# Metering the background matmuls by PSUM group, earlier modulation rows, and a branch place of its own for each engine, in a fused adaLN attention and MLP kernel

## The chip, the cores and the metric

The kernel runs on one NeuronCore of a Trainium2 chip. The metric is the device time of one execution in microseconds (us). Engines are named as the profile names them: PE (matmuls; PEld is its weight load), ACT, DVE, POOL, and SP, which here only issues DMAs.

## The reference, cut to what matters

A transformer block on 2048 rows of 512 values: a modulated layer norm, 32 query heads on 8 cached key/value heads over the last 512 cache positions, an output projection, a second modulated layer norm and a ReLU MLP. Six modulation vectors come from one small vector `c`.

```
mod = (silu(c) @ w_mod).reshape(6, 512)          # sa, ca, ga, sb, cb, gb
h = layernorm(x) * (1 + ca) + sa
q = (h @ wq) per head;  k, v = last 512 rows of the caches, one per 4 heads
o = softmax(q k^T / sqrt(128)) v
x = x + ga * (concat(o) @ wo)                    # wo: 4096 x 512
h = layernorm(x) * (1 + cb) + sb
return x + gb * (relu(h @ w1) @ w2)              # w1: 512 x 1792
```

## The kernel before, in words

**Units and steps.** The rows are cut into four blocks of 512. A unit `u` is one head of one block, 128 in all. A program loop over steps `s` (line 1588 on) writes the instructions of all engines in order; no scheduler moves them later. In step `s` PE gets: half of the scores of unit `s` (`s_mms`, into psS), the query projection of unit `s+1` (`q_mms`, psQ), the other half of the scores, then probabilities times values for unit `s-1` (`pv_mms`, psO), then up to four pieces of background work (`pop_bg(4)`, line 1601). ACT copies the query projection out and takes the exponentials. DVE normalises each unit's output (`rinv`, then `o`, lines 1471 and 1472), and SP transposes it with a DMA into one of 22 buffers `oT`. Below, "pv of step s" is the sixteen psO matmuls that stand in step s.

**Background work.** Eight heads make a pass of the output projection. When unit `u` closes a pass, `wo_ready` gets it for step `u+2`, and `enqueue_wo` puts four groups on the queue `bgq`. A group is eight matmuls `psW<-wo,oT`, one for each head, that accumulate in the one PSUM bank psW, followed by an evacuation: DVE copies or adds psW into `acc` (lines 1492 and 1494). Each entry of `bgq` is one matmul, or one evacuation (in the set `evacs`). `mods2`, called at step 20, puts the rest of the modulation there: a row of four matmuls and its copy to `gaf`, one entry of 32 one-column matmuls and its copies to `modc`, and another row and its copy to `gbf`. They all use psW too. Because psW is one bank, a new group's first matmul waits until DVE has emptied it.

`pop_bg(n)` counts matmul entries only; evacuations are free, and it goes on after one:

```
while bgq and (n > 0 or bgq[0] in evacs):
    f = bgq.popleft()
    f()
    n -= f not in evacs
```

**Loads.** `add(step, fn)` puts a load or a layer-norm piece at a step. SP issues its DMAs in program order, and one that has to wait holds all behind it. The modulation weights 2 to 5 are loaded at steps 9, 11, 13 and 15 (line 1572). At steps 60 and 64 the MLP weights are loaded, each in two halves into the space of the modulation weights; the second half is a later writer of the same space and waits for the first to land. The layer norm of blocks 2 and 3 and the second layer norm of blocks 0 and 1 run close to each other and share `xn` and `xnT`.

**The tail.** The MLP is a list `mlp` of groups: `h1_group` (four matmuls into one of the four psS banks, then ACT's ReLU) and `y_group` (fourteen matmuls into psQ or psO, then two DVE operations and the output DMA). After the loop, the left background work and the last pass are mixed with the first `h1` groups, then come the last layer norm and the check value `flag` (line 1652). At line 1678 the place is noted at which all five engines branch: each waits for `flag`, loads it into a register (line 1718), compares and branches (line 1719) either to a general kernel, which did not run here, or to the rest of the fast kernel, which stands behind the general one.

Of the kernel before, what the change touches and what calls it, by code (L numbers as in the profile page):

```python
# [1197 lines left out]
def build_fast(nc, es, top, A_x, A_k_cache, A_v_cache, A_wq, A_wo, B_x, B_w1, B_w2, c, w_mod, out, flag):  # L1198
# [9 lines left out]
    NB = Sq // QB  # L1208
# [71 lines left out]
    kb = KB(nc)  # L1280
    PE = kb.stream("pe", sem("s_pe"))
    ACT = kb.stream("act", sem("s_act"))
    DVE = kb.stream("dve", sem("s_dve"))
    POOL = kb.stream("pool", sem("s_pool"))
    SP = kb.stream("sp", sem("s_sp"))
# [6 lines left out]
    def dma(out_ap, in_ap, key, reads=(), writes=(), transpose=False, eng=None):  # L1292
        k = dsem(key)
        if transpose:
            return kb.op(SP, lambda e: e.dma_start_transpose(out_ap, in_ap), reads=reads, writes=writes, dma_sem=k)
        return kb.op(eng or SP, lambda e: e.dma_start(out_ap, in_ap), reads=reads, writes=writes, dma_sem=k)  # L1296
# [13 lines left out]
    R_rinv, R_vmax, R_chk, R_good, R_flag = Res("rinv"), Res("vmax"), Res("chk"), Res("good"), Res("flag")  # L1310
# [22 lines left out]
    def load_wm(sl, eng=None):  # L1333
        dma(wm[sl], w_mod[:, sl * D:(sl + 1) * D].rearrange("(c p) n -> p c n", p=P), f"wm{sl}", writes=[R_wm[sl]], eng=eng)
# [100 lines left out]
    def pop_bg(n):  # L1435
        while bgq and (n > 0 or bgq[0] in evacs):
            f = bgq.popleft()
            f()
            n -= f not in evacs

    evacs = set()

# [4 lines left out]
    def q_mms(u):  # L1447
        b, h = units[u]
        order = CC_ORDER if u == 0 else range(DC)
        for i, cc in enumerate(order):  # L1450
            mm(bank[QBK], wq_sb[:, cc, h * Dh:(h + 1) * Dh], hT[b % 2][:, cc, :], i == 0, i == DC - 1,
               [R_wq[h], R_hT[b % 2][cc]], [QBK], i == DC - 1)
        kb.op(ACT, lambda e: e.activation(qT[u % NQT][:, :], bank[QBK], ACTF.Copy), reads=[R_b[QBK]], writes=[R_qT[u % NQT]])  # L1453

    def s_mms(u, pr):
        b, h = units[u]
        g = h // R
        for i in range(2):
            kc = pr * 2 + i
            mm(s_ps[pr][:, i, :], kT_sb[:, g, kc * P:(kc + 1) * P], qT[u % NQT][:, :], True, True, [R_kT[g], R_qT[u % NQT]], [kc], i == 1)  # L1460
        kb.op(ACT, lambda e: e.activation(PT[u % NPT][:, pr * 2:pr * 2 + 2, :], s_ps[pr][:, :, :], ACTF.Exp, scale=scale),  # L1461
              reads=[R_b[pr * 2], R_b[pr * 2 + 1]], writes=[R_PT[u % NPT][pr]])
# [43 lines left out]
    def add(step, fn):  # L1506
        tasks.append((step, len(tasks), fn))
        tasks.sort(key=lambda x: x[:2])

    def run_tasks(step, n):  # L1510
        while tasks and tasks[0][0] <= step and n > 0:
            tasks.pop(0)[2]()
            n -= 1
# [55 lines left out]
    for j in range(NPASS):  # L1569
        add(HQ * j + 4, lambda j=j: load_wo(j))  # L1570
    for i, sl in enumerate((2, 3, 4, 5)):
        add(9 + 2 * i, lambda sl=sl: load_wm(sl))
    for b in range(1, NB):
        add(H * b - 20, lambda b=b: load_x(b))
        add_ln(b, 1, H * b - 15)
# [5 lines left out]
    def mods2():  # L1581
        mod_row(0)
        fs = mod_cols_mm(1, WBK)
        bgq.append(lambda: [f() for f in fs] and None)
        evac(lambda: mod_cols_evac(1, WBK))
        mod_row(1)

    for s in range(NU):
        run_tasks(s, 100)
        if s == 20:  # L1590
            mods2()
        if wo_ready and wo_ready[0][0] <= s:
            _, b_, j_ = wo_ready.popleft()
            enqueue_wo(b_, j_)
        s_mms(s, 0)
        if s + 1 < NU:
            q_mms(s + 1)
        s_mms(s, 1)
        if s >= 1:
            pv_mms(s - 1)  # L1600
        pop_bg(4)
# [5 lines left out]
    def h1_group(b, fc):  # L1607
        dst, r = h2_of[b]
        bk = hb_banks[cnt["h"] % len(hb_banks)]
        cnt["h"] += 1  # L1610
        for cc in range(DC):
            mm(bank[bk], w1_sb[:, cc, fc * P:(fc + 1) * P], dst[:, cc, :], cc == 0, cc == DC - 1, [R_w1[fc], r[cc]], [bk], cc == DC - 1)
        kb.op(ACT, lambda e: e.activation(h1T[b % 2][:, fc, :], bank[bk], ACTF.Relu), reads=[R_b[bk]], writes=[R_h1[b % 2][fc]],  # L1613
              pre=all_events(R_wq) if b < 2 else ())

    def y_group(b, tl):
        pt_done = all_events(R_PT[0] + R_PT[1])
        t = b * TPB + tl
        bk = yb_banks[cnt["y"] % len(yb_banks)]
        i = cnt["y"] % NY  # L1620
        cnt["y"] += 1
        for fc in range(FC):
            mm(bank[bk], h1T[b % 2][:, fc, tl * P:(tl + 1) * P], w2_sb[:, fc, :], fc == 0, fc == FC - 1, [R_h1[b % 2][fc], R_w2[fc]], [bk], fc == FC - 1)
        kb.op(DVE, lambda e: e.tensor_tensor(yt[i], bank[bk], gbf[:, :], op=ALU.mult), reads=[R_b[bk], R_gb], writes=[R_yt[i]], pre=pt_done if cnt["y"] <= NY else ())  # L1624
        kb.op(DVE, lambda e: e.tensor_tensor(yo[i], yt[i], x_sb[:, t, :], op=ALU.add), reads=[R_yt[i], R_x[t]], writes=[R_yo[i]])  # L1625
        dma(ov[:, t, :], yo[i], f"y{i}", reads=[R_yo[i]])

    mlp = deque()
    for b in range(NB + 1):
        if b < NB:  # L1630
            mlp.extend(lambda b=b, fc=fc: h1_group(b, fc) for fc in range(FC))
        if b >= 1:
            mlp.extend(lambda b=b, tl=tl: y_group(b - 1, tl) for tl in range(TPB))

    def pop_mlp(n):
        for _ in range(n):
            if mlp:
                mlp.popleft()()
# [27 lines left out]
    b = NB - 1  # L1666
# [7 lines left out]
        ln_norm(b * TPB + tl)  # L1674
    ln_dmaT()
    flag_mm()
    pop_mlp(4)
    cut = {n: (len(t.ops), t.cnt) for n, t in (("sp", SP), ("pe", PE), ("act", ACT), ("dve", DVE), ("pool", POOL))}
    cut_dma = dict(kb.dma_cnt)
    pop_mlp(4)  # L1680
    for cc in range(DC):
        ln_mod_sb(cc, *h2_of[b], 2)
    while mlp:
        pop_mlp(1)
    assert not tasks and not bgq and not wo_ready
    SP.ops.append((lambda e: e.nop(), [(f"y{i}", kb.dma_cnt[f"y{i}"]) for i in range(NY)], []))
    return kb, {"sp": SP, "pe": PE, "act": ACT, "dve": DVE, "pool": POOL}, cut, cut_dma, R_flag.w


def bass_adaLN_cond__sliding_block_cached__dense_activation_relu__prompt_kernel(  # L1690
    nc: bass.Bass,
    A_x: bass.AP,
    A_k_cache: bass.AP,
    A_v_cache: bass.AP,
    A_wq: bass.AP,
    A_wo: bass.AP,
    B_x: bass.AP,
    B_w1: bass.AP,
    B_w2: bass.AP,
    c: bass.AP,  # L1700
    w_mod: bass.AP,
    out: bass.AP,
):
    args = (A_x, A_k_cache, A_v_cache, A_wq, A_wo, B_x, B_w1, B_w2, c, w_mod, out)
    with ExitStack() as top:
        flag = top.enter_context(nc.sbuf_tensor("flag", [1, 8], mybir.dt.int32))
        with ExitStack() as es:
            kb, fast, cut, cut_dma, flag_ev = build_fast(nc, es, top, *args, flag)
            sems = dict(kb.sems)
            meet = top.enter_context(nc.semaphore("s_meet"))  # L1710
        with ExitStack() as es:
            gkb, general = build_general(nc, es, *args)

            def engine(name, e):
                n_ops, n_done = cut[name]
                kb.emit(fast[name], e, 0, n_ops)
                e.wait_ge(sems[flag_ev[0]], flag_ev[1])
                v = e.value_load(flag[0:1, 0:1])
                with e.If(v != 128):
                    if n_done:  # L1720
                        e.wait_ge(sems[name], n_done)
                    if name == "sp":
                        for k, n in cut_dma.items():
                            e.wait_ge(sems[k], n)
                    e.sem_inc(meet, 1)
                    e.wait_ge(meet, len(cut))
                    gkb.emit(general[name], e)
                with e.Else():
                    kb.emit(fast[name], e, n_ops)

            with nc.allow_non_contiguous_dma(reason="tiny c vector load in column layout, value rows of 256 bytes"):
                with nc.Block() as block:
                    @block.sync
                    def _(e):
                        engine("sp", e)

                    @block.tensor
                    def _(e):
                        engine("pe", e)

                    @block.scalar
                    def _(e):
                        engine("act", e)

                    @block.vector
                    def _(e):
                        engine("dve", e)

                    @block.gpsimd
                    def _(e):  # L1750
                        engine("pool", e)
    return nc
# [28 lines left out]
```

## Time and profile before

| What | us |
|---|---|
| median of 3 runs | 658.51 (658.41 to 659.48) |
| the profiled execution, its own time | 660.11 |
| span in its trace, first to last instruction | 658.4 |
| outside the span | 1.7 |
| PE busy in the span | 565.7 (86%) |
| ACT busy / DVE busy / POOL busy | 347.4 / 240.7 / 38.1 |

The engines run side by side, so the columns are not added up. The idle time that stands behind a group of instructions, and what ended it, say where an engine waited; on PE, whose work forms most of the chain that ended last, such a wait is a part of the span. A row of the timeline gives start and duration in us, the engine, the line, the tiles, the count, and in brackets the idle time before it with what ended it.

### The profile page before, as it was taken

What the parts mean: (1) busy time and instruction counts of PE and PEld (TensorE: products, weight loads), DVE (VectorE), ACT (ScalarE), POOL (GpSimd) and SP (SyncE); (2) the same over time, 40 slices, a digit from 0 to 9 for tenths busy, and PEclk for the clock granted to TensorE, in tenths of its full rate; (3) what the DMA queues carried; (4) which work ended last, traced back from release to release, by engine and by line L of the source; (5) the groups of instructions that cost most, each with busy time, mean ns of one, the idle gap of its engine ahead of it and who ended that gap; (6) DMA issues with size and microseconds to landing.
All of it is one profiled execution on the core that took longest, in us unless ns stands there. A gap on an engine that the chain in (4) does not pass through costs nothing.

```text
span 658.4 us, 9730 instructions
## 1 busy us (share of the span) xinstructions
PE 565.7 (86%) x4157; PEld 315.2 (48%) x4157; DVE 240.7 (37%) x531; ACT 347.4 (53%) x445; POOL 38.1 (6%) x40
## 2 busy tenths in 40 slices
PE   3999998888888888888888888888888879699997
PEld 3566555444444445544444444444454444244443
DVE  3343654222225443222235442222233325430324
ACT  1887665555555555555555555555555543415220
POOL 1000000002200100012100000022000000000000
PEclk9999999999999999999999999999999999989999
DMA  9299583111221245511211511111112310300001
GB/s 231 42 206 271 125 176 85 44 32 33 38 60 32 42 81 143 144 33 28 62 33 32 97 33 33 33 27 30 33 33 33 63 27 8 37 18 16 33 16 49
DMA packets 111620, 42.67 MB, mean 65 GB/s; under 512 B 94032, under 2 KB 111184, under 8 KB 111568
## 3 DMA queue, kind: packets, MB, share of 16 engines
q1 hardware_dynamic: 109984, 40.92, 29.1%
q10 hardware_dynamic: 1584, 1.05, 0.5%
q8 instruction: 34, 0.56, 0.4%
q14 instruction: 18, 0.15, 0.1%
HBM read 18.35 MB, written 2.10 MB: 31 GB/s over the span
## 4 chain that ended last, share of the span: by engine, by line
PE 84%; DVE 11%; issue 3%; DMA 1%; ACT 0%; ACTq 0%
PE psS L1350 25%; PE psO L1350 22%; PE psQ L1350 20%; PE psW L1350 17%; DVE o L1472 4%; DVE acc L1494 4%; DVE rinv L1471 2%; DVE acc L1492 1%; DMA wmw<-in_w_mod_dram 1%; PE psS L1353 0%; ACT qT L1453 0%; ACT PT L1461 0%; ACTq L1296 0%; DVE PT L1624 0%; DVE PT L1625 0%
## 5 line engine op out<-in xcount | busy, mean ns | idle before, releaser
L1461 ACT ACTIVATE PT<-psS 128x1024 bf16<-128x1024 f32 x256 | 262.7, 1027 | 207.6 <-PE psS L1350 207.5
L1350 PE MATMUL psW<-wo,oT 128*128 128x512 bf16 x512 | 139.3, 380 | 71.5 <-DVE acc L1494 53.5
L1350 PE MATMUL psS<-qT,kT 128*128 128x512 bf16 x512 | 152.1, 379 | 1.1 <-ACT qT L1453 1.1
L1350 PEld LDWEIGHTS psO<-v,PT 128*128 128x128 bf16 x2048 | 126.6, 98 | 30.2
L1471 DVE RECIPROCAL rinv<-psO 128x4 f32<-128x4 f32 x128 | 23.4, 183 | 317.1 <-PE psO L1350 317.1
L1350 PE MATMUL psO<-v,PT 128*128 128x129 bf16 x2048 | 137.0, 220 | 0.0
L1350 PE MATMUL psQ<-hT,wq 128*128 128x512 bf16 x512 | 131.6, 379 | 0.7 <-DVE hT L1397 0.7
L1350 PEld LDWEIGHTS psW<-wo,oT 128*128 128x128 bf16 x512 | 42.9, 98 | 116.1 <-DVE acc L1494 66.0
L1472 DVE TENSOR_TENSOR o<-psO,rinv 128x512 bf16<-128x512 f32 x128 | 88.5, 691 | 4.5
L1350 PEld LDWEIGHTS psQ<-hT,wq 128*128 128x128 bf16 x512 | 50.1, 98 | 61.4 <-issue 0.9
L1350 PEld LDWEIGHTS psS<-qT,kT 128*128 128x128 bf16 x512 | 49.6, 98 | 59.9 <-issue 1.0
L1453 ACT ACTIVATE qT<-psQ 128x512 bf16<-128x512 f32 x128 | 75.7, 591 | 0.5 <-PE psQ L1350 0.5
L1613 ACT ACTIVATE wq<-psS 128x512 bf16<-128x512 f32 x56 | 33.4, 597 | 61.8 <-PE psS L1350 61.8
L1494 DVE TENSOR_TENSOR acc<-psW,acc 128x512 f32<-128x512 f32 x48 | 32.7, 681 | 9.1 <-PE psW L1350 9.1
L1350 PE MATMUL psS<-h2T,wmw 128*128 128x512 bf16 x112 | 28.6, 411 | 5.1 <-issue 5.1
L1350 PE MATMUL psO<-wmw,wq 128*128 128x512 bf16 x140 | 31.2, 379 | 0.0
L1497 POOL TENSOR_TENSOR acc<-acc,gaf 128x512 f32<-128x512 f32 x12 | 15.2, 1266 | 246.4 <-DVE acc L1494 246.4
L1350 PE MATMUL psS<-hT,wmw 128*128 128x512 bf16 x112 | 24.5, 379 | 0.0
L1366 POOL TENSOR_TENSOR rstd<-rstd,cst 128x4 f32<-128x4 f32 x8 | 8.1, 1013 | 281.6 <-DVE rstd L1365 281.6
L1360 DVE BATCH_NORM_STATS2 st<-x 128x6 f32<-128x512 bf16 x32 | 21.7, 677 | 1.5 <-DMA x<-in_A_x_dram 1.5
L1624 DVE TENSOR_TENSOR PT<-psO,gbf 128x512 f32<-128x512 f32 x10 | 6.9, 691 | 40.2 <-PE psO L1350 40.2
L1350 PEld LDWEIGHTS psO<-wmw,wq 128*128 128x128 bf16 x140 | 13.7, 98 | 16.5
(57 smaller groups left out, 163.5 us busy)
## 6 DMA issues: line engine op xcount, KB each, us to landing
wo<-in_A_wo_dram SPq DMA_DIRECT2D x4, 1024.0 KB, 6.1
wq<-in_A_wq_dram SPq DMA_DIRECT2D x7, 512.0 KB, 4.8
wmw<-in_B_w_dram SPq DMA_DIRECT2D x4, 896.0 KB, 5.2
oT<-o SPq DMA_TRANSPOSE x128, 2.4
wmw<-in_w_mod_dram SPq DMA_DIRECT2D x4, 512.0 KB, 5.8
out_dram<-PT SPq DMA_DIRECT2D x16, 128.0 KB, 1.7
x<-in_A_x_dram SPq DMA_DIRECT2D x3, 512.0 KB, 4.2
wmw<-in_w_mod_dram ACTq DMA_DIRECT2D x2, 512.0 KB, 7.3
```

The costliest lines, as they stand in the source:

```text
L1350: kb.op(PE, lambda e: e.matmul(out_ap, lhsT, rhs, start=start, stop=stop), reads=reads, group_writes=[R_b[k] for k in bk], signal=signal)
L1360: kb.op(DVE, lambda e: e.bn_stats(st[:, t, :], x_sb[:, t, :]), reads=[R_x[t]], writes=[R_st[t]])
L1366: kb.op(POOL, lambda e: e.tensor_tensor(rstd[:, sl], rstd[:, sl], cst[:, 0:1].to_broadcast([P, TPB]), op=ALU.pow), reads=[R_rstd[b], R_cst ...
L1453: kb.op(ACT, lambda e: e.activation(qT[u % NQT][:, :], bank[QBK], ACTF.Copy), reads=[R_b[QBK]], writes=[R_qT[u % NQT]])
L1461: kb.op(ACT, lambda e: e.activation(PT[u % NPT][:, pr * 2:pr * 2 + 2, :], s_ps[pr][:, :, :], ACTF.Exp, scale=scale), reads=[R_b[pr * 2], R ...
L1471: kb.op(DVE, lambda e: e.reciprocal(rinv[:, u, :], o_ps[:, :, P]), reads=[R_b[5], R_b[6]], writes=[R_rinv])
L1472: kb.op(DVE, lambda e: e.tensor_tensor(o_sb[u % NOS][:, :, :], o_ps[:, :, 0:P], rinv[:, u, :].unsqueeze(2).to_broadcast([P, TPB, P]), op=A ...
L1492: kb.op(DVE, lambda e: e.tensor_copy(acc[:, tl, :], bank[WBK]), reads=[R_b[WBK]], writes=[R_acc[tl]])
L1494: kb.op(DVE, lambda e: e.tensor_tensor(acc[:, tl, :], bank[WBK], acc[:, tl, :], op=ALU.add), reads=[R_b[WBK], R_acc[tl]], writes=[R_acc[tl]])
L1497: kb.op(eng, lambda e: e.tensor_tensor(acc[:, tl, :], acc[:, tl, :], gaf[:, :], op=ALU.mult), reads=[R_acc[tl], R_ga], writes=[R_acc[tl]])
L1613: kb.op(ACT, lambda e: e.activation(h1T[b % 2][:, fc, :], bank[bk], ACTF.Relu), reads=[R_b[bk]], writes=[R_h1[b % 2][fc]], pre=all_events( ...
L1624: kb.op(DVE, lambda e: e.tensor_tensor(yt[i], bank[bk], gbf[:, :], op=ALU.mult), reads=[R_b[bk], R_gb], writes=[R_yt[i]], pre=pt_done if c ...
```

## The change

Three places change in the order, and the branch with them.

`pop_bg` now counts an evacuation as an entry and stops behind it. The four modulation weights are loaded at steps 0 to 3, and `mods2` is called at step 4. Each engine notes its own branch place inside the MLP list: ACT behind the third block's `h1` groups, PE between the second and the third `y` group of the second block, DVE, SP and POOL behind that block's last `y` group. So the rest of the fast kernel now stands in both arms of the branch; in the general arm it runs first.

```
         while bgq and (n > 0 or bgq[0] in evacs):
             f = bgq.popleft()
             f()
-            n -= f not in evacs
+            n -= 1
+            if f in evacs:
+                break
...
     for i, sl in enumerate((2, 3, 4, 5)):
-        add(9 + 2 * i, lambda sl=sl: load_wm(sl))
+        add(i, lambda sl=sl: load_wm(sl))
...
-        if s == 20:
+        if s == 4:
             mods2()
...
+    def cut_here(name):
+        cut[name] = len(streams[name].ops)
...
     for b in range(NB + 1):
         if b < NB:
             mlp.extend(lambda b=b, fc=fc: h1_group(b, fc) for fc in range(FC))
+            if b == NB - 2:
+                mlp.append(lambda: cut_here("act"))
         if b >= 1:
             mlp.extend(lambda b=b, tl=tl: y_group(b - 1, tl) for tl in range(TPB))
+            if b == NB - 2:
+                mlp.insert(len(mlp) - 2, lambda: cut_here("pe"))
+                mlp.extend(lambda n=n: cut_here(n) for n in ("dve", "sp", "pool"))
...
-    pop_mlp(4)
-    cut = {n: (len(t.ops), t.cnt) for n, t in (("sp", SP), ("pe", PE), ("act", ACT), ("dve", DVE), ("pool", POOL))}
-    cut_dma = dict(kb.dma_cnt)
-    pop_mlp(4)
+    pop_mlp(8)
...
             def engine(name, e):
...
                 with e.If(v != 128):
-                    if n_done:
-                        e.wait_ge(sems[name], n_done)
+                    kb.emit(stream, e, n_ops)
+                    if stream.cnt:
+                        e.wait_ge(sems[name], stream.cnt)
...
                 with e.Else():
-                    kb.emit(fast[name], e, n_ops)
+                    kb.emit(stream, e, n_ops)
```

How the rows of PE move inside the loop. Before, PE in steps 28 and 29; oT1 is the eighth head of a group there, and oT16 is the first of the next:

```order
L1350 MATMUL psW<-wo,oT19 128x512
L1350 MATMUL psW<-wo,oT20 128x512
L1350 MATMUL psW<-wo,oT21 128x512
L1350 MATMUL psW<-wo,oT0 128x512
L1350 MATMUL psS0<-qT1,kT 128x512 x2
L1350 MATMUL psQ<-hT0,wq 128x512 x4
L1350 MATMUL psS1<-qT1,kT 128x512 x2
L1350 MATMUL psO<-v,PT1 128x129 x16
L1350 MATMUL psW<-wo,oT1 128x512
L1350 MATMUL psW<-wo,oT16 128x512
L1350 MATMUL psW<-wo,oT17 128x512
L1350 MATMUL psW<-wo,oT18 128x512
```

Now, the same heads on PE:

```order
L1350 MATMUL psW<-wo,oT16 128x512
L1350 MATMUL psW<-wo,oT17 128x512
L1350 MATMUL psW<-wo,oT18 128x512
L1350 MATMUL psW<-wo,oT19 128x512
L1350 MATMUL psS0<-qT0,kT 128x512 x2
L1350 MATMUL psQ<-hT0,wq 128x512 x4
L1350 MATMUL psS1<-qT0,kT 128x512 x2
L1350 MATMUL psO<-v,PT1 128x129 x16
L1350 MATMUL psW<-wo,oT20 128x512
L1350 MATMUL psW<-wo,oT21 128x512
L1350 MATMUL psW<-wo,oT0 128x512
L1350 MATMUL psW<-wo,oT1 128x512
```

A group of eight was spread as 3, 4 and 1 over three steps, with the next group's three behind the 1; it is now 4 and 4 in two steps, and a step holds matmuls of one group only.

SP at the start, the change as a difference (`wmw<-in_w_mod_dram` are the modulation weights, `oT<-o` the transposes):

```order
 L1296 DMA v<-in_A_v_cache_dram 128x4x128
+L1296 DMA wmw<-in_w_mod_dram 128x4x512
 L1296 DMA wq<-in_A_wq_dram 128x4x512
 L1295 DMA_TRANSPOSE kT<-in_A_k_cache_dram 128x512
 L1296 DMA v<-in_A_v_cache_dram 128x4x128
-L1295 DMA_TRANSPOSE oT<-o 128x4x128 x3
+L1296 DMA wmw<-in_w_mod_dram 128x4x512
+L1295 DMA_TRANSPOSE oT<-o 128x4x128
+L1296 DMA wmw<-in_w_mod_dram 128x4x512
+L1295 DMA_TRANSPOSE oT<-o 128x4x128
+L1296 DMA wmw<-in_w_mod_dram 128x4x512
+L1295 DMA_TRANSPOSE oT<-o 128x4x128
```

One weight load now stands ahead of the loads of head group 2, and the other three stand among the first three transposes.

PE at its branch. Before, `ones,good` being the matmul that sums up the check:

```order
L1350 MATMUL psS<-h2T,wmw 128x512 x36
L1350 MATMUL psW<-ones,good 1x1
L1350 MATMUL psS<-h2T,wmw 128x512 x16
L1718 TENSOR_LOAD flag
L1719 COMPARE_AND_BRANCH
```

Now, where psQ and psO in groups of fourteen are `y` groups:

```order
L1350 MATMUL psS<-h2T,wmw 128x512 x36
L1350 MATMUL psW<-ones,good 1x1
L1350 MATMUL psS<-h2T,wmw 128x512 x40
L1350 MATMUL psQ<-wmw,wq 128x512 x14
L1350 MATMUL psO<-wmw,wq 128x512 x28
L1350 MATMUL psQ<-wmw,wq 128x512 x14
L1350 MATMUL psS<-hT,wmw 128x512 x56
L1350 MATMUL psO<-wmw,wq 128x512 x28
L1728 TENSOR_LOAD flag
L1729 COMPARE_AND_BRANCH
```

The branch stood 16 matmuls behind the check's matmul and stands 180 behind it now, directly behind two `y` groups.

More of the change, by code (lines that the diff above doesn't have):

```diff
@@ L1626, in y_group @@
         dma(ov[:, t, :], yo[i], f"y{i}", reads=[R_yo[i]])
+    cut = {}
+    def cut_here(name):
+        cut[name] = len(streams[name].ops)
+    streams = {"sp": SP, "pe": PE, "act": ACT, "dve": DVE, "pool": POOL}
     mlp = deque()
@@ L1686, in build_fast @@
     SP.ops.append((lambda e: e.nop(), [(f"y{i}", kb.dma_cnt[f"y{i}"]) for i in range(NY)], []))
-    return kb, {"sp": SP, "pe": PE, "act": ACT, "dve": DVE, "pool": POOL}, cut, cut_dma, R_flag.w
+    return kb, streams, cut, dict(kb.dma_cnt), R_flag.w
 def bass_adaLN_cond__sliding_block_cached__dense_activation_relu__prompt_kernel(
@@ L1707, in bass_adaLN_cond__sliding_block_cached__dense_activation_relu__prompt_kernel @@
         with ExitStack() as es:
-            kb, fast, cut, cut_dma, flag_ev = build_fast(nc, es, top, *args, flag)
+            kb, fast, cut, dma_cnt, flag_ev = build_fast(nc, es, top, *args, flag)
             sems = dict(kb.sems)
@@ L1714, in engine @@
             def engine(name, e):
-                n_ops, n_done = cut[name]
-                kb.emit(fast[name], e, 0, n_ops)
+                stream, n_ops = fast[name], cut[name]
+                kb.emit(stream, e, 0, n_ops)
                 e.wait_ge(sems[flag_ev[0]], flag_ev[1])
@@ L1719, in engine @@
                 with e.If(v != 128):
-                    if n_done:
-                        e.wait_ge(sems[name], n_done)
+                    kb.emit(stream, e, n_ops)
+                    if stream.cnt:
+                        e.wait_ge(sems[name], stream.cnt)
                     if name == "sp":
-                        for k, n in cut_dma.items():
+                        for k, n in dma_cnt.items():
                             e.wait_ge(sems[k], n)
                     e.sem_inc(meet, 1)
-                    e.wait_ge(meet, len(cut))
+                    e.wait_ge(meet, len(fast))
                     gkb.emit(general[name], e)
                 with e.Else():
-                    kb.emit(fast[name], e, n_ops)
+                    kb.emit(stream, e, n_ops)
             with nc.allow_non_contiguous_dma(reason="tiny c vector load in column layout, value rows of 256 bytes"):
```

## The prediction, as put on record before the result was known

> **What bounds the kernel now.** I read the chain that ended last, then the groups by idle time, then the waits of the main loop, then its timeline. The chain and the group of the output projection:
>
> ```profile
> PE 84%; DVE 11%; issue 3%; DMA 1%; ACT 0%; ACTq 0%
> ...
> L1350 PE MATMUL psW<-wo,oT 128*128 128x512 bf16 x512 | 139.3, 380 | 71.5 <-DVE acc L1494 53.5 <-DVE acc L1492 16.6 <-DVE gbf L1431 1.5
> ```
>
> PE is the chain, broken by 11% of DVE and 3% of "issue". One group of PE instructions has nearly all of PE's idle time in front of it: the matmuls into psW, which wait for DVE to empty that bank. The waits of PE from step 27 to the loop's end (us in total, times, longest):
>
> ```profile
> PE psW L1350 <- DVE acc L1494: 51.3, 37, 1.5
> PE psW L1350 <- DVE acc L1492: 16.6, 12, 1.4
> PE psW L1350 <- DVE gbf L1431: 1.5, 1, 1.5
> ```
>
> There are 50, one in every second step, and nothing else. The timeline of PE, then of DVE, in steps 28 to 30:
>
> ```profile
> 112.50 1.07 PE L1350 MATMUL psO<-v,PT 128*128 128x129 bf16 x16
> ...
> 116.00 1.07 PE L1350 MATMUL psO<-v,PT 128*128 128x129 bf16 x16
> 116.90 0.38 PE L1350 MATMUL psW<-wo,oT 128*128 128x512 bf16 x1
> 118.67 0.82 PE L1350 MATMUL psW<-wo,oT 128*128 128x512 bf16 x3 [1.39 <-DVE acc L1494]
> 119.32 0.59 PE L1350 MATMUL psS<-qT,kT 128*128 128x512 bf16 x2
> ...
> 121.05 1.07 PE L1350 MATMUL psO<-v,PT 128*128 128x129 bf16 x16
> ```
>
> ```profile
> 117.10 0.18 DVE L1471 RECIPROCAL rinv<-psO 128x4 f32<-128x4 f32 x1 [2.59 <-PE psO L1350]
> 117.32 0.69 DVE L1472 TENSOR_TENSOR o<-psO,rinv 128x512 bf16<-128x512 f32 x1
> 117.93 0.68 DVE L1494 TENSOR_TENSOR acc<-psW,acc 128x512 f32<-128x512 f32 x1
> ```
>
> PE closes a group with one matmul at 116.90 and wants to open the next at once, but DVE has rinv and o in front of the evacuation and ends it at 118.61. DVE itself is not late: it had idled 2.59 us. The wait comes from where the next group stands. Before step 25 the queue happened to hold whole groups in pairs of steps; the background work of steps 9 and 25 starts at:
>
> ```profile
> 44.11 1.03 PE L1350 MATMUL psW<-wo,oT 128*128 128x512 bf16 x4
> ...
> 100.06 1.03 PE L1350 MATMUL psW<-wmw,sc_rep 128*128 128x512 bf16 x4
> ```
>
> That is 55.95 us for 16 steps, 3.497 each. The same step with its four background matmuls costs 3.497 where groups are aligned, and a pair costs 121.05 - 112.50 = 8.55 where they aren't. From here I take steps 9 to 24 as the model of the changed loop.
>
> **The metered queue.** It removes the 50 waits. Each costs 8.55 - 2 x 3.497 = 1.56 us (the idle 1.39 and the drain of the last matmul): 50 x 1.56 = 78.0. No matmul is added or lost. What is late next in such a step? DVE's evacuation ends about 1.7 us after the group's last matmul begins (118.61 - 116.90), and the next group's first matmul now comes 2.63 us of other matmuls later (3.497 less four of 0.217), so nothing. After step 26 and behind the loop three more such waits stand, with the last pv of the loop as a mark:
>
> ```profile
> 104.98 0.82 PE L1350 MATMUL psW<-wmw,sc_rep 128*128 128x512 bf16 x3 [0.49 <-DVE modc L1425]
> ...
> 534.18 1.07 PE L1350 MATMUL psO<-v,PT 128*128 128x129 bf16 x16
> ...
> 536.85 1.90 PE L1350 MATMUL psW<-wo,oT 128*128 128x512 bf16 x8 [1.39 <-DVE acc L1494]
> ...
> 539.53 0.82 PE L1350 MATMUL psW<-wo,oT 128*128 128x512 bf16 x3 [0.79 <-DVE acc L1494]
> ```
>
> Now a group's end is followed by scores, or by two h1 groups, so 0.49, 1.39 and 0.79 go as well, each with some 0.15 of drain: 3.1. The metered queue is worth **81.1 us**.
>
> **The earlier modulation rows.** Same instructions, moved from steps 25 to 27 into steps 4 to 6, where the queue was empty; that is what keeps the later groups aligned. Four loads of 512 KB pass to SP's early queue. The transposes there, the landing time of such loads, and pv of step 4:
>
> ```profile
> 24.18 6.46 SPq L1295 DMA_TRANSPOSE oT<-o  x3
> ...
> DMA to landing us min/median/max: 5.0/5.7/8.1
> ...
> 30.04 1.07 PE L1350 MATMUL psO<-v,PT 128*128 128x129 bf16 x16
> ```
>
> SP goes from the first transpose (24.18, some 1.2 to issue) to the third load, 25.4, which lands between 30.4 and 33.5. The one-column matmuls want it in step 5, at 30.04 + 3.50 + 0.90 = 34.4. The fourth load, 28.0, lands by 36.1 and is wanted in step 6, at about 38. So 0, but the cover is 0.9 us; a later landing would cost its whole excess, since PE works in order. Taking the loads from steps 9 to 15 gains nothing: those steps had no wait.
>
> **What the shorter lag uncovers.** Before, nine matmuls of modulation delayed every group by over two steps. Now the eighth head of a pass is multiplied two steps behind its own pv, and its transpose must have landed. SP in steps 63 to 64, pv of step 63, and the landing of the last transpose shown:
>
> ```profile
> 261.43 1.07 PE L1350 MATMUL psO<-v,PT 128*128 128x129 bf16 x16
> ```
>
> ```profile
> 263.48 1.19 SPq L1295 DMA_TRANSPOSE oT<-o x1
> 264.71 5.74 SPq L1296 DMA_DIRECT2D wmw<-in_B_w_dram  x2
> 270.50 1.25 SPq L1295 DMA_TRANSPOSE oT<-o x1
> ```
>
> ```profile
> DMA to landing us min/median/max: 5.5/5.5/5.5
> ```
>
> The second half of an MLP weight load waits 5 us for the first, and the transpose of unit 63, the eighth head of its pass, is queued behind it. It lands at 276.0. With steps of 3.497 its matmul would come at 261.43 + 3 x 3.497 + 0.90 + 3 x 0.22 = 273.5: a new wait of **2.5 us**, once (step 60 does the same to a head that is not the last). And where two layer norms meet:
>
> ```profile
> 235.56 1.99 SPq L1295 DMA_TRANSPOSE xnT<-xn  x1
> ```
>
> ```profile
> 236.89 0.18 DVE L1471 RECIPROCAL rinv<-psO 128x4 f32<-128x4 f32 x1 [1.95 <-PE psO L1350]
> ...
> 239.94 0.42 DVE L1379 TENSOR_SCALAR hT<-xnT,modc 128x512 bf16<-128x512 bf16 x1 [1.54 <-DMA xnT<-xn]
> ```
>
> DVE waits for the transposed rows, and the next step's rinv is queued behind. In the changed order an evacuation stands ahead of this transpose's inputs, so it is issued about with rinv of step 57 and lands 4.4 us later; two hT follow, and the next rinv comes 5.1 us after the last instead of 3.5. DVE has some 1.5 us of slack before PE wants psO, so 0.2 to 0.4 us are left, twice: **0.8 us** (0 to 3, if it lands a microsecond later).
>
> **The branch.** Flag, PE's branch, and what came behind it:
>
> ```profile
> 569.03 0.14 DVE L1652 CAST flag<-psW 1x1 int32<-1x1 f32 x1
> ```
>
> ```profile
> L1719 PEldq COMPARE_BRANCH  x1: 4922/4922/4922, 569.8 to 569.8; - x1
> ```
>
> ```profile
> 574.74 7.45 PE L1350 MATMUL psS<-h2T,wmw 128*128 128x512 bf16 x20 [5.15 <-issue]
> ```
>
> ```profile
> 574.74:582.19 7.45, 7.45 (x21) 2.82 (x22) 1.38 (x4) 2.39 (x4) 0.00 (x0) 0.60 0.07 13
> ```
>
> PE idled 5.15 us, from flag to first matmul 5.57, and then the granted clock was 0.60 of full in this stretch: 20 matmuls took 7.45 instead of 20 x 0.217 = 4.34 (0.217 from 118.67 to 119.32 for three). Together 8.3 us. The work is the same in the new place. But there the flag is old, and the last 28 matmuls ahead of the branch wait for nothing new, so the sequencer can be ahead of the array when it branches. How far? PE's code comes in blocks (queue q8), each fetched as the sequencer moves on. Blocks and executed matmuls plus weight loads in two stretches:
>
> ```profile
> 128.45:540.90 412.45, 345.18 (x2695) 198.17 (x2693) 142.34 (x326) 232.64 (x287) 34.10 (x29) 1.00 0.24 49
> ...
> 66.05:343.39 277.34, 237.94 (x1888) 137.65 (x1887) 102.74 (x232) 161.32 (x200) 22.39 (x19) 1.00 0.32 70
> ```
>
> ```profile
> q8 instruction: 21, 0.34, 0.4%
> ```
>
> ```profile
> q8 instruction: 15, 0.25, 0.4%
> ```
>
> 5388 instructions for 21 blocks is 257 each, but only 3775 for 15, 252 each: by the second stretch's end the sequencer was some 70 instructions further ahead than at its start, some 30 matmuls, or 30 x 0.217 = 6.5 us. That exceeds 5.57. Bounds: nothing of the 8.3 saved, or all. I take 0.5 left, 7.8 saved, being nearer to the fetch rows. The other engines' branches lie under at least 12 us of PE work. [...]
>
> **The sum.** 81.1 + 7.8 - 2.5 - 0.8 = 85.6. The span goes from 658.4 to 572.8, and the profiled execution (660.1, 1.7 of it outside the span) to 574.5. The median of the runs is 658.5, 1.6 below that execution; so 658.5 - 85.6 = **572.9 us**.
>
> **Rivals.**
> - *The forecast*, 70%: 569.1 (no new wait, nothing left at the branch: 658.5 - 81.1 - 8.3) to 577.
> - *The branch is only moved*, 20%: if the sequencer has no lead when it fetches, PE idles 5.15 and runs slow again: 572.9 + 7.8 = 580.7. For it: the only branch in the trace was fully paid. Against: there PE's sequencer stood waiting for the flag. [...]
> - *A wait for transposes takes the old one's place*, 7%: if the eighth head's transpose came 2 us late in 15 passes, 572.9 + 30 = 603. Against: steps 9 to 24 had this lag and no such wait.
> - *Slower*, 2%: if a loop without PE idle time lowered the granted clock. It decides at a mean clock of 572.9 / 658.5 = 0.87 in the whole kernel; at 0.85, 674. Against: 1.00 in both stretches above.
> - *The queue is not aligned after all*, 1%: 658.5. Against: the rows of PE shown with the change.
>
> A measurement of this kernel tells about 0.2% (1.3 us) from no change. Only the last two rivals are not faster: 0.97, 0.01, 0.02. The range runs from 569 to 582, the branch rival with 1.3 us more for the later transposes; it leaves out the last three, a tenth.
>
> **What would show it.** psW waiting for acc: near 0 us instead of 71.5. Steps of 3.50 throughout, one wait of 2.5 on a transpose near step 66. No gap and no slow clock behind PE's branch; a gap of 5 there makes the second rival right. It is wrong if steps are longer than 3.6 or psW waits for DMA in many passes.

## The result and the profile after

The changed kernel takes 574.89 us (574.68 to 575.09, 4 runs) against 659.0 before (658.41 to 660.05); the ratio is 0.8722 [0.8707, 0.8737]. The forecast was 572.9, in a range of 569 to 582. The profiled span fell from 658.4 to 573.3. The page's chain, and all that PE waited for (us in total, times, longest):

```profile
PE 94%; DMA 3%; issue 1%; ACT 1%; DVE 0%; SPq 0%; ACTq 0%
```

```profile
PE psQ L1350 <- DMA wmw<-in_w_mod_dram: 9.8, 1, 9.8
PE psW L1350 <- DMA oT<-o: 2.5, 1, 2.5
PE psS L1350 <- ACT qT L1455: 1.1, 2, 0.8
PE psQ L1350 <- ACT hT L1400: 0.9, 1, 0.9
PE psQ L1350 <- issue: 0.4, 1, 0.4
```

DVE has gone from the chain (11% before), and no matmul waits for `acc` any more. The 9.8 is the start, as before. One wait in the loop is new, 2.5 us for a transposed head, and the branch has left 0.4.

The loop's first pv (step 1) and its last (step 127), in the timeline of PE:

```profile
21.64 1.07 PE L1350 MATMUL psO<-v,PT 128*128 128x129 bf16 x16
...
461.33 1.07 PE L1350 MATMUL psO<-v,PT 128*128 128x129 bf16 x16
```

and the first one before:

```profile
22.14 1.07 PE L1350 MATMUL psO<-v,PT 128*128 128x129 bf16 x16
```

The loop took 534.18 - 22.14 = 512.04 before and 439.69 now, 72.4 less. From its last pv to the end of the span it was 124.2 and is 112.0, 12.2 less. The start came out 0.5 shorter; over all ten traces step 1's pv begins anywhere from 21.6 to 23.1, so half a microsecond of any span says nothing. That is the whole 85.1.

The one wait, in the timeline of PE at steps 66 and 67:

```profile
244.55 1.07 PE L1350 MATMUL psO<-v,PT 128*128 128x129 bf16 x16
245.45 0.81 PE L1350 MATMUL psW<-wo,oT 128*128 128x512 bf16 x3
248.75 0.46 PE L1350 MATMUL psW<-wo,oT 128*128 128x512 bf16 x1 [2.49 <-DMA oT<-o]
249.00 1.06 PE L1350 MATMUL psS<-qT,kT 128*128 128x512 bf16 x2
249.85 1.91 PE L1350 MATMUL psQ<-hT,wq 128*128 128x512 bf16 x4
...
252.39 1.07 PE L1350 MATMUL psO<-v,PT 128*128 128x129 bf16 x16
```

SP around it, and the granted clock behind it (the stretch, its us, busy time of PE, PEld, DVE, ACT, POOL, then the clock):

```profile
237.33 5.87 SPq L1296 DMA_DIRECT2D wmw<-in_B_w_dram  x2
243.25 4.53 SPq L1295 DMA_TRANSPOSE oT<-o  x3
```

```profile
249.00:252.00 3.00, 3.00 (x9) 1.08 (x8) 0.69 (x1) 1.22 (x2) 1.91 (x2) 0.50 0.00 0
```

Three heads are multiplied and the eighth is waited for; its transpose stood behind the second half of the MLP weight load, issued at 243.25, and landed 5.5 us later. Then four query matmuls take 1.7 us instead of 0.86: the clock is at half. The step is 252.39 - 244.55 = 7.84 long, 4.34 over a clean 3.50. Every other step from 9 to 125 is 3.50 long.

The branch of PE, its duration in ns and its place, and the matmuls on both sides:

```profile
L1729 PEldq COMPARE_BRANCH  x1: 3808/3808/3808, 523.3 to 523.3; - x1
```

```profile
L1728 PEldq TENSOR_LOAD <-flag x1: 489/489/489, 522.8 to 522.8; - x1
```

```profile
520.61 6.21 PE L1350 MATMUL psO<-wmw,wq 128*128 128x512 bf16 x27
527.21 2.98 PE L1350 MATMUL psQ<-wmw,wq 128*128 128x512 bf16 x13 [0.39 <-issue]
```

The sequencer loads the flag at 522.8, while the array works through the two y groups until 526.8; it comes back at 527.1. The branch is still paid, 4.3 us of it, but under matmuls that were already queued. No slow clock follows: thirteen matmuls take 2.98.

### The profile page after: what moved, and what is told of

Its sections match the earlier page's. It is cut to its first block, busy times and chain, and to the rows that moved or that the text cites. A ratio compares the mean times of both kernels' runs of the same rounds, so it can differ in the third digit from the quotient of the medians.

```text
span 573.3 us, 9628 instructions
## 1 busy us (share of the span) xinstructions
PE 551.1 (96%) x4082; PEld 316.8 (55%) x4157; DVE 242.8 (42%) x531; ACT 347.7 (61%) x445; POOL 38.2 (7%) x40
## 4 chain that ended last, share of the span: by engine, by line
PE 94%; DMA 3%; issue 1%; ACT 1%; DVE 0%; SPq 0%; ACTq 0%
PE psS L1350 27%; PE psO L1350 25%; PE psQ L1350 22%; PE psW L1350 19%; DMA wmw<-in_w_mod_dram 1%; DMA wmw<-in_B_w_dram 1%; DMA oT<-o 1%; SPq L1295 0%; ACT qT L1455 0%; ACT PT L1463 0%; PE psS L1353 0%; ACTq L1296 0%; ACT hT L1400 0%; DVE PT L1626 0%; DVE o L1474 0%
## 5 line engine op out<-in xcount | busy, mean ns | idle before, releaser
L1350 PE MATMUL psW<-wo,oT 128*128 128x512 bf16 x451 | 118.0, 379 | 5.7 <-DMA oT<-o 2.5
L1350 PEld LDWEIGHTS psW<-wo,oT 128*128 128x128 bf16 x512 | 45.0, 98 | 35.7 <-DMA oT<-o 3.0
L1350 PE MATMUL psS<-h2T,wmw 128*128 128x512 bf16 x110 | 25.2, 379 | 0.1
```

Of the source, the lines that this page charges most:

```text
L1350: kb.op(PE, lambda e: e.matmul(out_ap, lhsT, rhs, start=start, stop=stop), reads=reads, group_writes=[R_b[k] for k in bk], signal=signal)
```

## The experiments

My theory: the waits came only from a group that began in the step in which the last one ended, and PE's branch is hidden by the sequencer's lead. The rivals stand with each run. The kernel before ran beside them at 659.5 to 660.0 us.

**Metering alone, on the kernel before.**

```
-            n -= f not in evacs
+            n -= 1
+            if f in evacs:
+                break
```

> The kernel before with the metered queue alone; rows and loads of the modulation and the branch as before. Theory: the waits at psW come only from a group that begins in the step in which the last one ended, so metering alone removes the 50 waits of 1.56 us in the loop, the 0.65 of the modulation and one of the two behind the loop (0.95; behind step 127 a group still follows directly): 658.5 - 79.6 = 578.9 us. The groups keep a lag of three steps, so no wait for a transpose at step 66, and the branch still costs 8.3. Rival: the rows had to leave the middle of the loop for the groups to fall into pairs of steps; then some of the waits stay and the time is over 600.

Measured: 579.45 us, ratio 0.8794 [0.8778, 0.8810]. Its waits on PE:

```profile
PE psS L1350 <- issue: 5.1, 1, 5.1
...
PE psW L1350 <- DVE acc L1496: 0.8, 1, 0.8
```

The 50 waits are gone without the rows being moved; the branch costs its 5.1 as before, and the one wait between two groups behind the loop is there. No wait for a transpose: the groups still lag by three steps. The rival is out.

**The changed kernel with the old count.** The same four lines, undone.

> The changed kernel with the old count in the queue; the modulation rows stay in steps 4 to 6, the branch places stay new. Theory: it is the alignment that matters, and with the rows out of the way groups of eight fall into pairs of steps under the old count too; only one wait of 0.5 (0.65 with its drain) for modc comes back in step 5: 574.9 + 0.65 = 575.5 us. Rival: the metering is what removed the waits, and with the old count 50 of them come back: about 653 us.

Measured: 576.21 us, ratio 0.8730 [0.8712, 0.8749], whose interval overlaps that of the changed kernel.

```profile
PE psW L1350 <- DMA oT<-o: 2.1, 1, 2.1
...
PE psW L1350 <- DVE modc L1425: 0.7, 1, 0.7
```

The waits for `acc` do not come back, and the rival is out. With the modulation rows out of the way, groups of eight matmuls fall into pairs of steps under the old count as well. So either edit alone removes the waits, and neither adds to the other: it is the alignment.

**The branch places alone, on the kernel before.** Only `cut_here`, the moved cuts and `emit` in both arms, as in the diff above.

> The kernel before with the new branch places alone. Theory: PE's sequencer runs ahead of the array in the y groups and pays its branch while queued matmuls run; idle 5.15 becomes about 0.4 and the slow clock behind it (3.1) goes: 658.5 - 7.9 = 650.6 us. Rival: the branch is paid wherever it stands, and the gap was short in the changed kernel for another reason: 658.5 us.

Measured: 652.02 us, ratio 0.9889 [0.9874, 0.9905]: 7.3 us of 658.5, where 7.9 was expected. PE at the branch:

```profile
597.40 6.21 PE L1350 MATMUL psO<-wmw,wq 128*128 128x512 bf16 x28
604.16 2.98 PE L1350 MATMUL psQ<-wmw,wq 128*128 128x512 bf16 x13 [0.55 <-issue]
```

The gap is short in the long kernel too, and the rival is out.

**The second MLP weight at step 65.**

```
-    add(64, load_w2)
+    add(65, load_w2)
```

> The changed kernel with the load of the second MLP weight put at step 65 instead of 64, so that the transpose of unit 63 stands ahead of it on SP. Theory: the one wait of the loop, in step 66 (2.5 us, and then 3.4 us at half clock, together 4.3), goes with all that follows from it: 574.9 - 4.3 = 570.6 us. Rival: the slow clock has nothing to do with this wait, so that only 2.5 is saved: 572.4. Second rival: the transposes of units 64 and 65, now behind the load, come late instead: 574.9 or more.

Measured: 571.39 us, ratio 0.8663 [0.8650, 0.8675]. Of the five waits of the changed kernel's PE, the one on `oT` is gone and no other took its place:

```profile
PE psS L1350 <- ACT qT L1455: 1.1, 2, 0.8
PE psQ L1350 <- ACT hT L1400: 0.9, 1, 0.9
PE psQ L1350 <- issue: 0.5, 1, 0.5
```

3.5 us by the medians and 0.0059 of 658.5, 3.9, by the ratios: between the two values expected (4.3 with a slow clock each time, 2.5 without), which fits what the next runs show of that clock. This is the lowest median of all versions, though its interval overlaps that of the last run below.

**PE's branch back at its old place, the other four new.** `cut_here("pe")` four h1 groups behind the check's matmul.

> The changed kernel with PE's branch alone put back to where it stood, 16 matmuls behind the check's matmul; the other four engines keep their new places. Theory: PE's own wait for the flag leaves its sequencer no lead there, so that its load of the flag and its branch (0.5 and 3.8 to 4.9 us) are idle time again, 4.2 to 5.1, with the slow clock behind it: 574.9 + 7 to 8 = 582 to 583 us. Rival: the gap was long because all five engines fetched their code at once; with PE alone there it is under 3 us and the clock stays: under 578.

Measured: 580.53 us, ratio 0.8795 [0.8780, 0.8810]. PE behind the branch, the clock there, and the branch:

```profile
495.08 8.11 PE L1350 MATMUL psS<-h2T,wmw 128*128 128x512 bf16 x23 [4.33 <-issue]
```

```profile
495.08:503.03 7.95, 7.89 (x24) 3.08 (x26) 1.38 (x4) 2.98 (x5) 0.00 (x0) 0.65 0.04 10
```

```profile
L1730 PEldq COMPARE_BRANCH  x1: 4102/4102/4102, 490.9 to 490.9; - x1
```

Gap and slow clock are back with PE alone at the old place; five engines at the branch at once are not the cause, though the branch took 4.1 here and 4.9 when all five took it together. The time is 1.5 to 2.5 under the expectation. In this execution step 66 waited as long, with no slow clock behind it, which is 1.7 us of that (4.34 - 2.49 less the drain of 0.15):

```profile
249.76 0.39 PE L1350 MATMUL psW<-wo,oT 128*128 128x512 bf16 x1 [2.47 <-DMA oT<-o]
```

```profile
250.00:253.00 3.00, 2.95 (x26) 1.88 (x26) 0.87 (x2) 2.38 (x3) 1.96 (x2) 1.00 0.00 0
```

**PE's branch two y groups earlier.**

```
-                mlp.insert(len(mlp) - 2, lambda: cut_here("pe"))
+                mlp.insert(len(mlp) - 4, lambda: cut_here("pe"))
```

> The changed kernel with PE's branch two y groups earlier, directly behind the h1 groups of the third block. There the sequencer has to wait for ACT to empty a bank four groups back, which comes about 2.6 us before the array ends the last group. Theory: the lead is set by the last wait ahead of the branch; with 2.6 us of lead and a branch of 4.3, PE idles about 1.8 and the time is 574.9 + 1.4 = 576.3 us. Rival: the lead is there in any case as long as the flag is old: 574.9 and a gap of 0.4.

Measured: 575.82 us, ratio 0.8722 [0.8707, 0.8736]; the time can't tell it from the changed kernel: whether the clock falls behind step 66 is worth 1.7 us, and mean clocks from 0.997 to 1.000 among the executions of both say that it did in some of them only. The trace can tell:

```profile
523.56 6.22 PE L1350 MATMUL psO<-wmw,wq 128*128 128x512 bf16 x27 [1.22 <-issue]
```

```profile
L1728 PEldq TENSOR_LOAD <-flag x1: 484/484/484, 519.6 to 519.6; - x1
```

```profile
L1729 PEldq COMPARE_BRANCH  x1: 3369/3369/3369, 520.1 to 520.1; - x1
```

The array ended at 523.56 - 1.22 = 522.34, so the lead was 2.7 us, as expected from the wait four banks back (2.6): ACT's evacuation four groups back ran from 518.93 to 519.53, and the flag was loaded at 519.6. The gap was 1.2 and not 1.8 because this branch took 3.4 us.

**The first MLP weight at step 48**, which puts the transpose of unit 47 behind a wait of SP as well.

```
-    add(60, load_w1)
+    add(48, load_w1)
```

> The changed kernel with the load of the first MLP weight put at step 48 instead of 60, so that the transpose of unit 47, the last head of its pass, is queued behind a second wait of SP. Theory: a second wait of 2.5 us at step 50, each followed by 3.4 us at half clock: 574.9 + 4.3 = 579.2 us. Rival: the slow clock after the wait was a chance of its moment, and only 2.5 is added: 577.4. Second rival: step 66 was late for another reason than SP's wait, and nothing is added: 574.9.

Measured: 579.03 us, ratio 0.8769 [0.8751, 0.8787]. SP at the new place, with the landing of the first transpose behind the load:

```profile
182.82 5.38 SPq L1296 DMA_DIRECT2D wmw<-in_B_w_dram  x2
188.24 12.08 SPq L1295 DMA_TRANSPOSE oT<-o  x4
```

```profile
DMA to landing us min/median/max: 6.8/6.8/6.8
```

The two waits of PE, and the clock behind each:

```profile
195.13 0.39 PE L1350 MATMUL psW<-wo,oT 128*128 128x512 bf16 x1 [3.38 <-DMA oT<-o]
...
253.59 0.39 PE L1350 MATMUL psW<-wo,oT 128*128 128x512 bf16 x1 [2.34 <-DMA oT<-o]
```

```profile
195.00:199.00 4.00, 3.82 (x29) 2.29 (x31) 3.01 (x7) 2.43 (x3) 0.00 (x0) 1.00 0.08 16
254.00:257.00 3.00, 3.00 (x16) 1.62 (x15) 0.69 (x1) 2.16 (x3) 2.14 (x2) 0.64 0.00 0
```

The second wait came, at the place and by the cause expected. The transpose landed at 195.0, and PE went on at 195.13. My theory of the clock fell: the wait of 3.38 left the clock at 1.00, the one of 2.34 halved it. That the time came out as forecast (579.2) is luck: the new wait was 0.9 longer than the 2.5 I took, and its slow clock did not come. The first rival was right that the length does not decide, but its time, 577.4, was not met either; the last section gives each wait with the clock behind it.

**The modulation rows back in the middle of the loop**, metering and branch places kept.

```
-        add(i, lambda sl=sl: load_wm(sl))
+        add(9 + 2 * i, lambda sl=sl: load_wm(sl))
...
-        if s == 4:
+        if s == 20:
```

> The changed kernel with the modulation rows and their loads put back to step 20 and steps 9 to 15; the metered queue and the new branch places stay. Theory: the earlier rows removed no wait that the metering does not remove, and by taking away the queue's lag they brought the wait of step 66 (4.3 with its slow clock). Without them that wait goes and one wait of about 1.6 between two groups behind the loop comes: 574.9 - 4.3 + 1.6 = 572.2 us, faster than the changed kernel. Rival: the early rows carry a part of the gain of their own; then it is 575 or more.

Measured: 572.25 us, ratio 0.8679 [0.8667, 0.8691], under the changed kernel's interval; as expected. The wait behind the loop is there, though it is 0.8 long and not 1.6, and the one on `oT` is not:

```profile
PE psS L1350 <- ACT qT L1455: 1.1, 2, 0.8
PE psW L1350 <- DVE acc L1496: 0.8, 1, 0.8
```

So the three parts, added in this order, by the ratios and 658.5 us: metering alone 79.4 faster, the branch places alone 7.3 faster, the earlier rows on top of both 0.0043 or 2.8 slower. Their sum, 83.9, agrees with the 84.2 of the whole change. In another order the shares would differ: without the metering, the rows would have removed the same waits.

## Why the prediction was right, and where it was not

- *The metered queue, 81.1.* Right in mechanism and size. The loop lost 72.4 although the new wait cost 4.34 in it, and although nine matmuls of background work moved into it from behind its end. The counts of weight loads into psW, the second number in brackets, show that; before, then now, from the loop's first pv to its last:

```profile
22.14:534.18 512.04, 130.53 (x503) 40.07 (x503) 40.45 (x61) 1.00 0.33 69
21.64:461.33 439.69, 111.74 (x452) 42.93 (x512) 42.42 (x63) 1.00 0.40 78
```

  Nine times 0.217 is 2.0, so the waits that went are 72.4 + 4.3 + 2.0 = 78.7, as forecast (78.0 and 0.65). Of the 12.2 behind the loop, the same 2.0 is work that moved; the other 10.2 are the two waits there (2.5 with their drain) and the branch. Steps 9 to 24 were the right model: each step is 3.50. One point was not seen: the earlier rows alone would have aligned the groups, so the 81.1 did not need the metering.
- *The earlier rows, 0.* Their own columns and rows cost nothing: the loads landed in 3.8 to 5.6 us, not 8.1, and PE did not wait in steps 4 to 6. Their price was the lag that they took away, which the prediction had under what the shorter lag uncovers. Whether the early loads also delay the start is not shown: step 1's pv begins at 21.6 to 23.1 in the six traces with early rows, at 21.6 to 22.3 in the four without.
- *The new wait at step 66, 2.5.* Right in place, cause and length (2.49). Mis-sized by what follows: the step lost 4.34, since 3.4 us at half clock came behind it (1.7 lost, and 0.15 of drain). The prediction had a slow clock only behind a gap like the branch's 5.15.
- *The two meeting layer norms, 0.8.* Wrong in size: 0. The queued rinv did come late behind the hT pair, but the transpose was issued 1.0 us ahead of the rinv at 214.18 and not with it, so the rows landed earlier than I had them, and DVE's slack covered the rest. SP, then DVE:

```profile
213.15 2.00 SPq L1295 DMA_TRANSPOSE xnT<-xn  x1
```

```profile
217.53 0.73 DVE L1379 TENSOR_SCALAR hT<-xnT,modc 128x512 bf16<-128x512 bf16 x2 [2.44 <-DMA xnT<-xn]
218.18 0.17 DVE L1473 RECIPROCAL rinv<-psO 128x4 f32<-128x4 f32 x1
218.39 0.69 DVE L1474 TENSOR_TENSOR o<-psO,rinv 128x512 bf16<-128x512 f32 x1
```

  psO was empty at 219.1; the next pv began at 220.07.
- *The branch, 0.5 left.* Right (0.39), partly by luck. I read a lead of some 30 matmuls out of the code blocks (70 instructions are 35, as each matmul has a weight load); the trace shows 526.8 - 522.8, 4.0 us or 18 matmuls, and with the branch places alone it was 4.0 as well. It nearly sufficed because flag load and branch together took 4.3 instead of 5.57. Why the block count gave too much was not tested; the block that I counted from may have come late. The 4.0 us put the sequencer some 36 instructions ahead (18 matmuls with their weight loads), with nothing to wait for.
- *The sum.* The span was to be 572.8 and is 573.3: 1.8 more at step 66, 0.8 less at the layer norms, 0.1 less at the branch and 0.5 less at the start. The median is 2.0 above the forecast; at the same before of 658.5 the ratio gives 574.3. One step of the sum explains most of it: the 85.6 was read off an execution of 660.11 and taken from a median of 658.5. Between the two profiled executions the change is 660.11 - 575.08 = 85.0. The 3.1 us of slow clock behind the branch was in that execution, whose mean clock was 0.995, but likely not in full in the median: of 25 executions of the kernel before beside the experiments, ten show 0.997, some 1.3 us less lost to the clock.

## What to carry to other kernels

A wait in front of an accumulation group can be cured by where the group starts, as 50 waits, 69.4 us together, were here; a faster evacuation was not needed, and not tried. Look for a stretch of the same kernel in which groups and steps are aligned, and take its step length as the forecast. Work that seems to be in the way can be a lag that something else needs; before it is moved, follow the queue whose results it gave time to. A long branch cost PE only what it took beyond the work that its sequencer had queued: 0.39 and 0.55 us with a lead of 4.0, 1.22 with 2.7, and 4.33 to 5.15 where the sequencer had waited for the flag itself.

## What the runs showed of the hardware that was not expected

PE's granted clock fell to half behind idle times of 2.13 us (the changed kernel with the old count, where the sixteen psO matmuls behind it took 1.83 instead of 1.07), 2.34 (first weight at step 48, 0.64 from 254 to 257) and 2.49 (the changed kernel, 0.50). It stayed at 1.00 behind 2.47 (branch at its old place), 3.38 (step 48) and the waits of 1.39 of the kernel before. The run with the branch two y groups earlier, whose wait was 2.8, had the same mean clock, 0.997, as the three in which it fell. The length of the gap does not decide alone.

The half-clock stretch was 3.4 us long in the changed kernel (248.94 to 252.36, at 0.50) and 6.8 in the kernel before (573.94 to 580.76, at 0.50), where the branch's gap was 5.15. Two traces have a gap that left the clock full and a fall elsewhere. The falls, in the run at step 48 and in the one with the branch at its old place (a stretch of 0.05 us each, the clock is the third number from the end):

```profile
254.80:254.85 0.05, 0.05 (x2) 0.00 (x0) 0.00 (x0) 0.05 (x1) 0.05 (x1) 0.83 0.00 0
493.85:493.90 0.05, 0.00 (x0) 0.00 (x0) 0.00 (x0) 0.00 (x0) 0.00 (x0) 0.72 0.09 10
```

The clock fell at 254.83, 1.24 us after the wait of 2.34 had ended (253.59), and at 493.87, 3.12 us into the branch's gap of 4.33 (490.75 to 495.08). In the changed kernel it fell at 248.94, 0.19 us after the wait of 2.49 had ended (248.75). What decides beside the length of the gap is not shown: no run set a gap's place.
